# A fused FFT and two MLP layers: another order of all steps, and some tiles placed 8 bytes further on

## The chip, the cores and the metric

The program runs on one core of one Trainium2 chip. The metric is the device time of one execution in microseconds (us); lower is better. Engines are named as in the profile: PE is TensorE's matmul pipe and PEld its weight loads, DVE is VectorE, ACT is ScalarE, POOL is GpSimd, and SP is SyncE, which issues nearly all DMAs.

## The reference

```python
X = fft(fft(x, axis=1), axis=2); x = X.real          # x: (2, 3008, 256), then as 6016 tokens of 256
h = x @ w_in                                          # 256 -> 2048
x = (h * clip(h + 3, 0, 6) / 6) @ w_out               # 2048 -> 256
xn = x / sqrt(mean(x * x) + 1e-6) * rms_g
g = xn @ w_gate; v = xn @ w_val                       # 256 -> 1536 each
out = ((g * sigmoid(g)) * v) @ w_out2                 # 1536 -> 256
```

Weights arrive as 64-bit floats and are decoded on the chip.

## The kernel before

Every product is made of numbers split in two: a high part, rounded to the matmul's format (`F32R`), and a low part, the rest. Three matmuls (high by high, high by low, low by high) make one product. The low part is a subtraction, original minus high part, and it is the bulk of what GpSimd does.

**Stages.** (1) The inputs are folded by symmetry (`fold`), the Fourier matrices converted (`conv_mat`) and multiplied (`pmm`, `xmm`); the second batch does the same later (`late_fold`, `late_split`, `group`). The weights of the first layer are decoded meanwhile (`dec_win`, `wmm`, `dec_wout`). (2) The first layer runs as 96 items: six blocks of 1004 tokens (two halves of 502), 16 groups of hidden columns each. One item is 6 matmuls into the PSUM banks E and O, three DVE operations, two ACT ones (`L619`), two DVE ones (`L622`), one ACT cast of the high part (`L625`), two subtractions of 502 columns (one for each half, recorded at `L342`, the line of the helper `sub`) and 12 matmuls into four accumulators (`L640`). Two items are in flight on two pairs of E and O banks, so an item's first matmuls wait until the item two before it has passed `L622`. (3) The second layer runs as 72 chunks: six blocks of 12. A chunk is seven products of 3 matmuls (`prod`, steps a to g, `L796`), which share two banks; `hold` (`L803`, ACT) and `plus` (`L809`, DVE) read partial sums out of the banks, then come silu, products (`times`, `L817`), the cast (`high`, `L824`), the subtraction (`lows`) and two output groups of 6 matmuls (`outs`, steps v and w, `L839`). Before a block its rows are normalized (`rms`) and split (`split_j`); the second layer's weights are decoded during the last third of stage 2 (`dec_w2`) and combined and split (`sum_w2`, `split_w2`).

**Order.** Every function is a generator that yields between its operations, and the string `STEPS` names, one step at a time, which generator goes on. Within an engine instructions run in the order of this list. A bare number is a step of an item; `37g` is step g of chunk 37; other names stand in `TASKS`. A prime matters where the step holds a subtraction, sum or product that goes through `low[0]`: with the prime it runs on DVE, without it on POOL:

```python
low[0] = V if step != task else G
```

**Layout.** A tile's tag is its slot in SBUF. The subtraction's original lies in tiles R0 to R2 (`[P, 2 * BL]`, two halves of 502 floats, so the second half starts 2008 bytes in), its high part in HI or LO tiles of `[P, 2, PB]` (PB = 504, second half 2016 bytes in). Decoded second-layer weights are staged in slots B0 and YB0 as four rows of 512 floats (`st`).

Of the kernel before, what the change touches and what calls it, by code (L numbers as in the profile page):

```python
# [24 lines left out]
BL = 502  # L25
# [89 lines left out]
    pq00 PQ110 mat12 dwo0 PQ111 mat12 pq00' dwo0 PQ012 mat12 dwo0' ev01 PQ112 ev01 dwi1 lwo1 0 ev11 dwi1 ev11 dwi1 1 0
    sx1 dwi1 sx1 sx1 0 dwi1 X10 1 0 dwi1 1 X11 lwi2 0 1 X12 lwi3 lwo3 wt1 0 1 pq01 0 2 evx1 1 0 evx1 wt1 dwo1 2 1 2 0
    wt1 1 wt1 wt1 dwo1 2 evx1 pq01 dwi3 2 1 dwi3 2 wt1 wt1 2 lwo2 3 g wt1 wt1 2 3 4 dwi3 2 3 dwi3 3 4 3 4 5 3 dwo1 3 4 5
    4 3 5 6 4 dwo1 4 5 3 6 dwo1 5 4 6 7 5 dwo1 6 7 7 5 4 dwi2 6 5 dwi2 7 8 dwi2 6 5 7 6 dwi2 6 9 8 7 8 7 6 9 8 7 9 8 9 7
    8 9 dwi2 8 10 9 8 7 11 10 9 10 9 8 11 10 dwi2 11 10 11 9 dwo2 11 10 dwo2 10 wt2 11 dwo2 12 10 g wt2 12 11 12 10 wt2
# [5 lines left out]
    28 26 27 25 26 28 28 26 29 lf1 27 lf2 28 27 26 29 28 27 29 30 28 lf2 29 28 27 30 29 28 30 31 29 30 29 28 31 31 29 30
    31 29 30 31 30 lf2 32 30 31 33 32 32 31 30 33 32 31 33 32 33 31 32 33 32 lf2 34 33 32 31 35 ls00 33 34 33 32 35 lf2
    34 lm01 35 33 34 ls00 35 34 35 34 36 34 35 gr00 36 34 36 35 36 34 35 ls10 36 gr00 lm02 ls10' gr00 37 36 36 38 37 37
    36 35 38 37 38 37 38 36 37 38 37 39 38 37 40 39 38 39 37 38 40 39 40 39 40 38 39 40 39 41 40 39 42 41 40 41 39 40 42
    41 42 41 42 40 41 42 41 43 42 41 44 43 42 43 41 42 44 43 44 43 44 42 43 44 43 45 44 43 gr10 45 44 45 44 45 43 lm10
    gr10 45 ls01 gr10 lm11 46 pq10 45 pq10' 47 45 46 44 47 45 46 ls01 47 46 45 47 46 47 46 48 46 47 gr01 48 47 48 46 47  # L130
    48 46 lm12 gr01 48 ls11 gr01 49 48 48 47 49 49 48 ls11' 49 50 gr01 gr01 gr01 gr01 gr01 gr01 lm12 lm12 lm12 lm12 lm12
    lm12 ls11 ls11 ls11 ls11 ls11 ls11 pq10 pq10 pq10 pq10 pq10 pq10 46 46 46 46 46 46 46 46 46 46 46 46 47 47 47 47 47
    47 47 47 47 47 47 47 49 50 48 48 48 48 48 48 48 48 48 48 48 48 49 50 49 50 50 49 gr11 lo00 lo00 50 lo10 lo10 rms0 50
    rms0' 51 gr11 50 rms0 gr11 gr11 gr11 gr11 pq11 49 49 49 49 49 49 49 49 rms0' 51 do00 pq11 pq11 pq11 pq11 pq11 51 51
    rms0 51 50 50 50 50 50 rms0 do10 rms0 51 do00 rms0 51 52 rms0' 53 51 52 52 51 51 51 51 52 rms0 52 rms0 rms0 53 52 54
    53 52 53 54 52 52 52 52 52 53 rms0 53 54 rms0 53 55 54 55 rms0 54 53 53 53 53 53 55 54 55 rms0 54 55 56 54 56 55 54
    54 54 54 56 55 56 56 55 57 rms0 56 rms0 rms0 rms0 55 55 55 55 56 57 rms1 57 56 57 rms1' 58 57 rms1 rms1 58 56 56 56
    56 57 58 57 58 58 57 rms1 57 57 57 57 do00 rms1 do10 58 rms1 58 rms1 59 rms1' 58 59 60 59 58 58 58 58 59 rms1 59
    rms1 rms1 60 59 61 60 59 60 61 59 59 59 59 59 60 rms1 60 61 rms1 60 62 61 62 rms1 61 60 60 60 60 60 62 61 62 rms1 61
    62 63 61 63 62 61 61 61 61 63 pq12 62 63 rms1 62 63 64 pq12 pq12 pq12 pq12 pq12 64 63 62 62 62 62 64 64 rms1 rms1  # L140
    rms1 hj00 63 64 65 hj01 63 65 64 63 65 hj00 hj00 65 65 64 63 63 63 66 sj01' 64 66 67 65 66 hj01 hj01 66 64 64 64 64
    67 65 66 65 67 sj03 67 65 65 65 65 67 66 do00 do00 hj04 66 hw07 lg00 lg00 68 67 hj04' hj04 66 68 66 66 66 66 68 67
    68 do10 dg00 67 68 69 69 hw07 hw07 68 67 67 67 67 69 68 69 69 68 70 do10 do10 69 70 lg10 lg10 hw08 68 68 68 68 69 70
    70 69 70 hw08 hw08 71 70 71 dg10 69 69 69 69 70 71 71 70 71 72 dg00 71 72 71 70 70 70 70 72 72 71 72 73 dg00 72 dg10
    71 71 71 71 72 73 73 72 73 dg00 dg00 74 73 hw00 lv00 lv00 hw00 hw00 74 72 72 72 72 73 74 73 74 74 73 dv00 75 dg10 74
    75 73 73 73 73 74 75 75 74 75 76 dg10 dg10 75 76 lv10 lv10 74 74 74 74 hw01 75 76 76 75 76 hw01 hw01 77 76 77 75 75
    75 75 dv10 dv00 76 77 77 76 77 78 dv00 77 76 76 76 76 78 77 78 78 77 78 79 dv00 dv00 78 79 77 77 77 77 lo01 lo01
    hj03 78 79 79 78 79 80 hj03 hj03 79 80 sj02 78 78 78 78 80 79 80 80 79 81 80 sj04' 81 hj05 80 79 81 81 80 81 79 79
    79 hj05 hj05 82 dv10 82 83 81 dv10 82 81 80 80 80 80 82 83 81 82 81 81 81 81 83 82 83 dv10 dv10 82 83 lo11 lo11 hw05
    84 82 83 84 82 82 82 82 83 84 84 83 84 hw05 hw05 85 84 85 sw01 83 83 83 83 85 84 hw03 85 sw03' 84 85 hw04 86 86 sw02  # L150
    85 84 84 84 84 86 hw04 hw04 hw02 86 sw04' 85 86 hw06 87 85 87 86 85 85 85 85 87 hw06 hw06 87 87 86 88 hw02' hw02 87
    86 88 86 86 86 86 88 87 88 hw03' hw03 87 88 hj06 hj02 89 hj06 hj06 88 89 87 87 87 87 hj02' hj02 88 89 do01 89 88 89
    do11 90 do01 89 88 88 88 88 90 89 90 90 89 90 91 do01 90 do11 89 89 89 89 90 91 91 90 91 92 do01 do01 do11 hw17 lg01
    lg01 91 90 90 90 90 hw17 hw17 92 91 do11 do11 91 92 lg11 lg11 93 92 91 93 91 91 91 91 dg01 92 dg01 92 93 dg11 92 94
    93 93 92 92 92 92 92 dg01 93 94 93 94 95 94 93 94 93 93 93 93 dg01 dg01 94 95 lv01 lv01 hw10 94 95 95 0a 94 95 0b
    hw10 hw10 1a 0h 95 0i 0c dg11 0d 0j 95 0k 1b dv01 0e dg11 94 94 94 94 0l 95 0m 1h dg11 dg11 1i hw11 lv11 lv11 dv01
    1j 0f hw11' hw11 0g 0n 1c 0o 0r 1d dv01 1k 95 0p 0s 0q 95 95 95 dv01 dv01 1e 0v 0t 1l 0u 1m 1f 0w 1n hw18 lo02 lo02
    1r hw18' hw18 1g 1s dv11 2a 1o 2b dv11 1p 1v 2h 1q 2i 1t 2c dv11 2j 1u 2d 2k 3a dv11 dv11 1w lo12 lo12 3h hw15 hw15'
    hw15 2e sw11' 3c 2l sw13' hw13 3b sw12' hw14 2f 2m hw13 hw13 3k hw12 2n 2g sw14' 2r 3e hw12' hw12 hw16 4a 2s 2o 3l
# [822 lines left out]
```

## Time and profile before

| | before |
|---|---|
| median of 3 runs | 1064.54 us (1064.09 to 1066.43) |
| the profiled execution | 1065.55 us, its span 1063.8 us |
| mean granted clock of TensorE | 0.992 |
| PE busy | 1010.9 us (95%), 4356 matmuls |
| DVE, ACT, POOL busy | 829.7, 667.7, 510.0 us |
| DVE, ACT, POOL instructions | 1278, 1081, 424 |

The span runs from the program's first instruction to its last; about 1.8 us of the profiled execution lie around it. A matmul's end is modelled, so PE's idle time and the pace of its starts say more than its busy share. Idle time of the other engines costs nothing by itself.

### The profile page before, as it was taken

To read this page: it belongs to the slowest core of one execution; us is meant where nothing else is said; L and a number is where in the kernel's file an instruction comes from. 1 tells how busy PE (TensorE), PEld (TensorE's weight loads), DVE (VectorE), ACT (ScalarE), POOL (GpSimd) and SP (SyncE) were. 2 spreads that over 40 slices of the span, in tenths; PEclk is the share of its full clock that TensorE was granted. 3 is DMA by queue.
4 is the path that set the end of the run, shared out by engine and by line. 5 is a ranking of instruction groups with operands and counts; after the bars stand their busy time and mean duration, and the time that the engine had idled before them with its cause. 6 is when DMAs were issued, how large, how long until landed. Compare 5 with 4: busy or idle time off the path is not lost.

```text
span 1063.8 us, 12508 instructions
## 1 busy us (share of the span) xinstructions
PE 1010.9 (95%) x4356; PEld 817.9 (77%) x4356; DVE 829.7 (78%) x1278; ACT 667.7 (63%) x1081; POOL 510.0 (48%) x424
## 2 busy tenths in 40 slices
...
GB/s 284 162 180 1 83 5 113 1 87 10 172 27 1 51 49 40 59 40 82 57 98 1 78 1 1 42 36 1 1 78 1 1 59 20 1 1 39 1 1 39
DMA packets 22119, 53.28 MB, mean 50 GB/s; under 512 B 4326, under 2 KB 9958, under 8 KB 21678
## 3 DMA queue, kind: packets, MB, share of 16 engines
...
## 4 chain that ended last, share of the span: by engine, by line
PE 63%; DVE 23%; ACT 4%; issue 4%; DMA 2%; POOL 2%; SPq 0%; POOLq 0%; DVEq 0%; ACTq 0%
PE E L796 17%; PE acc L839 16%; PE O L796 12%; PE acc L640 11%; DVE R L622 5%; DVE T L611 3%; PE E L607 3%; DVE E L613 3%; PE O L607 2%; DVE O L614 2%; POOL LO L342 1%; DMA J<-in_x 1%; DVE B L342 1%; ACT R L619 1%; ACT HI L625 1%
## 5 line engine op out<-in xcount | busy, mean ns | idle before, releaser
L342 POOL TENSOR_TENSOR LO<-R,HI 128x502 fp32r<-128x502 f32 x192 | 240.8, 1277 | 125.3 <-ACT HI L625 125.3
L640 PE MATMUL acc<-HI,B 128*128 128x502 f32 x768 | 249.8, 390 | 1.3 <-POOL B L342 1.2
L640 PEld LDWEIGHTS acc<-HI,B 128*128 128x128 f32 x768 | 144.6, 188 | 32.1 <-POOL B L342 1.6
L342 POOL TENSOR_TENSOR HI<-R,HI 128x502 fp32r<-128x502 f32 x72 | 86.9, 1208 | 171.6 <-ACT HI L824 101.6
L640 PE MATMUL acc<-LO,B 128*128 128x502 f32 x384 | 151.0, 393 | 3.8 <-POOL LO L342 3.8
L342 POOL TENSOR_TENSOR LO<-R,LO 128x502 fp32r<-128x502 f32 x72 | 88.2, 1225 | 127.4 <-ACT LO L824 58.9
L625 ACT CAST HI<-R 128x1004 fp32r<-128x1004 f32 x96 | 99.5, 1038 | 71.6 <-DVE R L622 49.4
L809 DVE TENSOR_TENSOR R<-R,O 128x502 f32<-128x502 f32 x144 | 96.3, 674 | 31.1 <-PE O L796 25.8
L813 ACT ACTIVATE R<-R 128x502 f32<-128x502 f32 x144 | 88.6, 623 | 45.7 <-DVE R L809 44.0
L619 ACT ACTIVATE R<-E,c_three 128x502 f32<-128x502 f32 x96 | 65.2, 679 | 81.3 <-DVE E L613 67.4
L607 PE MATMUL E<-J,A 128*128 128x502 f32 x288 | 84.1, 401 | 10.8 <-DVE R L622 8.1
L803 ACT COPY R<-E 128x502 f32<-128x502 f32 x144 | 82.0, 573 | 16.1 <-PE E L796 11.6
L640 PEld LDWEIGHTS acc<-LO,B 128*128 128x128 f32 x384 | 72.3, 188 | 22.0 <-POOL LO L342 7.3
L607 PE MATMUL O<-J,A 128*128 128x502 f32 x288 | 82.8, 396 | 0.3 <-DVE A L390 0.3
L809 DVE TENSOR_TENSOR T<-T,O 128x502 f32<-128x502 f32 x48 | 32.3, 673 | 54.8 <-ACT T L803 53.1
L607 PEld LDWEIGHTS E<-J,A 128*128 128x128 f32 x288 | 54.9, 194 | 25.8 <-DVE R L622 12.0
L824 ACT CAST LO<-R 128x502 fp32r<-128x502 f32 x72 | 44.1, 612 | 46.5 <-DVE R L817 46.1
L622 DVE SCALAR_TENSOR_TENSOR R<-R,E 128x502 f32<-128x502 f32 x96 | 64.5, 672 | 8.9 <-ACT R L619 8.8
L613 DVE TENSOR_TENSOR E<-T,O 128x502 f32<-128x502 f32 x96 | 65.6, 683 | 7.3
L614 DVE TENSOR_TENSOR O<-T,O 128x502 f32<-128x502 f32 x96 | 65.1, 678 | 0.0
L607 PEld LDWEIGHTS O<-J,A 128*128 128x128 f32 x288 | 55.3, 192 | 12.3 <-DVE A L390 0.7
L619 ACT ACTIVATE R<-O,c_three 128x502 f32<-128x502 f32 x96 | 64.5, 672 | 0.0
...
## 6 DMA issues: line engine op xcount, KB each, us to landing
...
```

Of the source, the lines that this page charges most:

```text
L342: low[0].tensor_tensor(o, a, b, op=ALU.subtract)
L607: T.matmul(bk[:, :BL], a[:, lw, eo, fs], j[:, eo, lx], start=(n == 0), stop=(n == 2))
L613: V.tensor_tensor(E[:, :BL], t, O[:, :BL], op=ALU.add)
L614: V.tensor_tensor(O[:, :BL], t, O[:, :BL], op=ALU.subtract)
L619: S.activation(x, bk[:, :BL], AF.Relu, bias=c3)
L622: V.scalar_tensor_tensor(x, x, 6.0, bk[:, :BL], op0=ALU.min, op1=ALU.mult)
L625: S.copy(hi, r.rearrange("p (h n) -> p h n", h=2))
L640: T.matmul(acc[k][:, :BL], w[:, lw, f % 4, d * P:(d + 1) * P], (hi, lo)[lx][:, hf], start=(first and n == 0), stop=(last and n == 2))
L796: T.matmul(bk[:, :BL], w[:, lw, fs], j[:, lx], start=(n == 0 and m in (0, 1, 3)), stop=(n == 2), skip_group_check=True)
L809: V.tensor_tensor(c["t"][m], c["t"][m], c["b", 1][:, :BL], op=ALU.add)
L813: S.activation(t, t, AF.Silu)
L839: T.matmul(acc2[p, m][d][:, :BL], w[:, lw, cs], h[:, lx], start=(f == 0 and n == 0), stop=(f == NF2 - 1 and n == 2))
```

## The change

All 3678 steps are the same ones and stand in another order; the engine of some subtractions and products changes with the primes. The list itself is too long to print; these are its start, the stretch around the first late fold and its end, in both versions. Late folds are `lf`; `lf0` and the beginning of `lf1` stand some items earlier.

```diff
 STEPS = """
-    one dm x01 x01 raw00 xq x00 x00 lwi0 raw01 raw02 x02 x02 raw11 raw10 fold1 fold1 fold1 fold1 fold1 mat00 mat00 fx
-    fold1 mat00 sx0 fold0 fold1 fold0 sx0 fold1' sx0 fold0 X00 fold1 fold0 fold1 fold0 dwi0 fold1' fold0 dwi0 fold0
+    one dm x00 x00 raw01 x01 x01 raw00 raw11 xq fold0 x02 fold0 fold0 x02 fold0 fold0 mat01 lwi0 fold0 mat01 mat01 fold1
+    raw02 fold0 fold1 fold0' raw10 fold1 fold1 fold1 mat00 g mat00 fold1 PQ000 mat00 fold0 fold1 PQ100 fx fold0 sx0
...
-    16 17 15 16 17 16 dwo3 18 16 17 19 dwo3 18 18 17 16 19 17 18 19 dwo3 18 19 17 18 19 18 lf0 20 19 18 21 20 lf0 19 18
-    21 20 19 21 20 19 lf0 21 20 x11 lf0 22 20 lf0 20 21 22 20 23 21 22 21 20 pq02 23 21 23 22 pq02 23 22 21 23 22 22 lf1
+    17 16 17 16 14 17 18 14 14 18 17 lf0 17 x11 15 18 lf0 lf0 19 16 19 17 16' 16 16 19 17 18 18 17 17 lf1 18 19 lf1 18
+    19 20 20 18 19 21 20 19 20 18 21 19 20 21 22 21 lf1 20 19 22 x12 20 21 20' 22 23 21 23 22 21 20 22 pq02 21' pq02 23
...
-    70g 70n 69w 70o 70r 70p 70s 71c 70q 71b 71k 70v 70t 71i 70u 71j 71d 70w 71e 71l 71m 71f 71g 71n 71o 71r 71s 71p 71v
-    71q 71t ev5o0 71u ev5o0 ev5o0 71w ev5o1 ev5o0 ev5o0 ev5o1 ev5o1 ev5o1 ev5o1
+    69g 71h 70g 69o 71c 70o 69p 71b 69q 70p 67v 71k 71i 70q 71j 71d 69r 71e 69s' 68v 71l 71m 71f 70r 69v 71n 70s 70v 71r
+    71s 71g 71v 71o 71p 67w ev5o0 71q ev5o0 ev5o0 68w 69t 69u' 69w 70t 70u' ev5o0 ev5o0 70w 71t 71u' 71w ev5o1 ev5o1
+    ev5o1 ev5o1 ev5o1
 """
...
-    xqt = sl("c_xq", [TC, NCH, 4, 4])
+    xqt = sl("c_p9", [TC, NCH, 4, 4])
...
-        r = sl(rr("R", 2), [P, 2 * BL])
-        rh = (r[:, :BL], r[:, BL:])
+        r = sl(rr("R", 2), [P, 2, PB])[:, :, 2:]
+        rh = (r[:, 0], r[:, 1])
...
-        S.copy(hi, r.rearrange("p (h n) -> p h n", h=2))
+        S.copy(hi, r)
...
-            stage[tag, c] = sl(tag, [P, 4, 512])
+            stage[tag, c] = sl(tag, [P, 4, 516])[:, :, 2:514]
...
-        sq = sl("H1" if p else "HI2", [P, 2, BL])
-        for k in range(2):
-            S.activation(sq[:, k], y[k], AF.Square)
-        yield
-        v, r = sq[:, 0], sq[:, 1]
+        sq = sl("H1" if p else "HI2", [P, 2 * BL + 2])
+        v, r = sq[:, 2:PB], sq[:, PB:]
+        for k, t in enumerate((v, r)):
+            S.activation(t, y[k], AF.Square)
+        yield
...
-            c["r"] = sl(RT[k % 3], [P, 2, BL])
+            c["r"] = sl(RT[k % 3], [P, 2, PB])[:, :, 2:]
```

Read off the two lists, operations that go through `low[0]`, old and new:

| kind | on DVE | on POOL |
|---|---|---|
| an item's two subtractions | 0 to 29 | 192 to 163 |
| a chunk's two subtractions (`lows`) | 0 to 68 | 144 to 76 |
| of `rms` | 49 to 23 | 11 to 37 |
| `split_j` and `split_w2` | 44 to 28 | 25 to 41 |
| first folds | 6 to 2 | 0 to 4 |
| the others | 29 to 29 | 29 to 29 |
| all | 128 to 179 | 401 to 350 |

DVE instructions that stand ahead of the first matmul of an item: of item 5 113 and now 111, of item 20 212 and now 222, of item 30 280 and now 287. Ahead of item 20 stood 1 instruction of a late fold and now 12. The matmuls ahead of items 20 and 30 are the same in number, 492 and 660. The DVE instructions from item 50 to item 95 are 289 and now 298, from chunk 18 to chunk 66 352 and now 375.

With the layout, both halves of R lie 8 bytes past a multiple of 16, counted from the slot's start (before: the first at 0, the second at 2008, which is 8 past one). The HI and LO tiles stay at 0 and 2016, both multiples of 16. The staged weights move from 0 to 8 past such a multiple, and so does v, the first operand of `rms`'s products.

## Rows read from the trace of the kernel before

**Rows 1.** Busy time of each engine by stretch; (x) instructions; PEclk granted clock.
```profile
core 0: us, PE busy (x) PEld busy (x) DVE busy (x) ACT busy (x) POOL busy (x), PEclk, DMA share, GB/s
95.00:225.00 130.00, 124.12 (x543) 101.04 (x542) 124.25 (x192) 77.81 (x109) 87.36 (x69) 1.00 0.20 50
300.00:480.00 180.00, 176.09 (x762) 142.46 (x762) 168.78 (x269) 118.99 (x171) 130.84 (x107) 1.00 0.11 36
480.00:625.00 145.00, 137.76 (x575) 107.05 (x574) 121.71 (x188) 100.39 (x176) 55.56 (x44) 0.99 0.18 58
625.00:1040.00 415.00, 414.99 (x1807) 337.56 (x1806) 264.97 (x390) 259.05 (x467) 155.39 (x132) 1.00 0.05 18
1040.00:1064.00 24.00, 17.10 (x70) 12.31 (x68) 10.38 (x14) 9.59 (x17) 7.03 (x6) 0.94 0.11 44
```

**Rows 2.** Waits of PE in 95:225, 300:480, 480:625, 1040:1064; total us, times, longest.
```profile
...
PE E L607 <- DVE R L622: 5.6, 5, 1.9
...
PE acc L640 <- POOL LO L342: 3.8, 7, 0.8
...
PE E L796 <- ACT R L803: 2.5, 3, 1.1
...
PE acc L839 <- POOL LO L342: 1.5, 2, 0.8
PE acc L839 <- ACT LO L824: 0.8, 1, 0.8
PE E L796 <- ACT c_p L803: 0.7, 1, 0.7
```

**Rows 3.** GpSimd by line and shape; busy us, mean ns, then idle before.
```profile
...
L342 POOL TENSOR_TENSOR W<-W 128x502 f32<-128x502 f32 x8 | 8.6, 1075 | 4.6 <-DVE W L342 4.6
...
L342 POOL TENSOR_TENSOR YB<-B,YB 128x512 fp32r<-128x512 f32 x4 | 5.2, 1294 | 0.0
```

**Rows 4.** Timeline of GpSimd in 312:318 and 655:668; start us, us.
```profile
...
312.14 1.27 POOL L342 TENSOR_TENSOR LO<-R,HI 128x502 fp32r<-128x502 f32 x1 [1.55 <-ACT HI L625]
313.38 1.27 POOL L762 TENSOR_TENSOR R<-R,HI 128x502 f32<-128x502 f32 x1
314.60 1.07 POOL L342 TENSOR_TENSOR LO<-R,HI 128x502 fp32r<-128x502 f32 x1
...
662.25 1.08 POOL L342 TENSOR_TENSOR LO<-R,LO 128x502 fp32r<-128x502 f32 x1
663.28 1.08 POOL L342 TENSOR_TENSOR W<-W 128x502 f32<-128x502 f32 x1
```

**Rows 5.** VectorE by line and shape, and its subtractions of L342 (min/median/max ns).
```profile
...
L817 DVE TENSOR_TENSOR R<-R,E 128x502 f32<-128x502 f32 x72 | 48.6, 675 | 17.6 <-PE E L796 17.5
L817 DVE TENSOR_TENSOR R<-R,c_p 128x502 f32<-128x502 f32 x24 | 24.4, 1015 | 11.0 <-ACT R L813 11.0
...
L342 DVE TENSOR_TENSOR J<-W,J x9: 668/682/683, 578.5 to 936.2; 128x502 fp32r<-128x502 f32 x9
```

**Rows 6.** ScalarE's cast of an item, and one that reads two runs (timeline).
```profile
...
L625 ACT CAST HI<-R 128x1004 fp32r<-128x1004 f32 x96 | 99.5, 1038 | 71.6 <-DVE R L622 49.4 <-PE acc L640 20.3 <-PE O L607 0.8
...
39.77 1.03 ACT L586 CAST J<-PQX 128x1004 fp32r<-128x1004 f32 x1 [1.07 <-DVE PQX L532]
```

**Rows 7.** Late folds on VectorE in 150:200, by line and shape.
```profile
...
L408 DVE TENSOR_TENSOR PQ<-PQ 126x1024 f32<-126x1024 f32 x3 | 4.4, 1453 | 0.0
L406 DVE TENSOR_TENSOR W<-PQ 126x1024 f32<-126x1024 f32 x3 | 3.9, 1316 | 0.0
...
L417 DVE TENSOR_TENSOR B<-W 126x256 f32<-126x256 f32 x8 | 3.0, 418 | 0.0
```

**Rows 8.** Two more stretches, columns as in the first group.
```profile
...
0.00:15.00 15.00, 0.73 (x2) 0.51 (x3) 7.78 (x21) 5.53 (x7) 0.94 (x5) 1.00 0.85 251
...
550.00:575.00 25.00, 23.53 (x93) 17.90 (x92) 22.81 (x36) 17.61 (x32) 8.23 (x7) 0.93 0.07 22
```

**Rows 9.** Timeline of TensorE at 560.
```profile
...
560.90 1.46 PE L796 MATMUL O<-B,B 128*128 128x502 f32 x3
```

More of the change, by code (lines that the diff above doesn't have):

```diff
@@ L115 @@
[L115 to L119, printed above, removed]
@@ L125 @@
[L125 to L129, printed above, removed]
@@ L130 @@
[L130 to L159, printed above, removed]
@@ L165 @@
-    dv12 dv12 6u hw25 rms2 ly1 ly1 7e rms2 hw25' hw25 6w 7l rms2 sw21' rms2 7f sw23' hw23 8a sw22' hw24 8b hw23' hw23
-    hw22 sw24' 8h hw22' hw22 hw26 8c hw24' hw24 8k hw26' hw26 8e rms2' 7m 8l rms2 7g 7n rms2 8f 7o 7r rms2 9a 8i 7p 9b
-    9h 7q 8d 8j 7s 9i 7t 9c 8m 9j 7v 7u 8n 9k 8r rms2 7w 8s rms2 rms2' 8g rms2 9d 8o 9e rms2 8p 8v rms2 rms2 rms2 9l
-    hj10 8q 9f rms3 9m hj10 hj10 10a 9n 8t 9g rms3' 9r 8u 10b 10h 9o rms3 10c 10i 9s 9p 8w 10j rms3' 10k 9q rms3 hj11
-    10d rms3 hj11' hj11 10e 9t rms3 9v 10l 9u rms3 10m 10f rms3' 9w rms3 10n rms3 10g 10r rms3' 11a 10s 10o 11b 10p rms3
@@ new lines @@
+    58 59 rms1 58 58 58 58 60 59 do10 do10 rms1 59 60 lg10 lg10 60 rms1 61 60 59 59 59 59 59 61 60 dg00 dg10 60 61 61 60
+    rms1 61 60 60 60 60 rms1 hw08 rms1 61 hw08' hw08 rms1 dg00 62 61 62 rms1 63 62 61 62 61 61 61 61 63 rms1 pq12 63
+    rms1 63 rms1 62 rms1 62 64 63 rms1 62 64 63 65 rms1 65 64 62 62 62 62 62 rms1 64 63 65 63 63 64 65 rms1 rms1 rms1
+    rms1 64 66 pq12' pq12 pq12 pq12 pq12 63 63 63 64 65 64 66 67 hj00 67 hj01 hj00 hj00 64 64 64 64 65 66 hj01 hj01 66
+    67 65 66 65 65 65 65 65 66 sj01' dg10 67 sj03 67 68 66 hj04 68 67 69 dg00 dg00 66 68 hw00 lv00 lv00 66 66 66 66 67
@@ new lines @@
+    68 69 68 67 69 hj04 hj04 67 67 67 67 68 hw00' hw00 dv00 68 69 69 68 70 70 69 68 68 68 68 dv00 69 70 70 69 70 71 dv00
+    70 72 71 70 71 69 69 69 69 71 70' 71 72 70 70 70 70 71 dg10 72 71 72 72 71 73 dg10 dg10 72 73 71 71 71 71 lv10 lv10
+    hw01 72 73 73 72 73 hw01 hw01 74 73 74 72 72 72 72 dv00 dv00 dv10 73 74 lo01 lo01 74 73' 74 75 75 74 73 73 73 73
+    dv10 74 75 75 74 75 76 76 75 74 74 74 74 dv10 75 76 76 75' 76 77 77 76 75 75 75 75 dv10 dv10 76 77 hw05 lo11 lo11 77
+    76 77 78 hw05 hw05 77 78 79 sw01' 77 78 hw03 76 76 76 76 78 77 79 78 hj03 hw03 hw03 79 hj03 hj03 77 77 77 77 78
@@ new lines @@
+    sw03' 79 sj02 79 hw04 78 80 79 sj04' 78 80 hj05 81 80 hj05 hj05 80 78 78 78 78 81 79 80 79 81 sw02 79 80 hw04' hw04
+    81 80 81 79 79 79 sw04 83 83 82 81 80' 83 hw02 81 80 80 80 80 83 82 81 83 hw06 hw02 hw02 82 81 81 81 81 83 hw06 hw06
+    82 83 82 hj06 84 hj02 hj06 hj06 82 84 85 83' 82 84 84 82' 82 82 82 82 85 84 85 83 83 83 83 85 hj02' hj02 85 do01
+    do11 86 do01 84 86 85 87 84 86 84 84 84 84 84 87 85 86 87 85 86 85 85 85 85 87 do01 87 86 do01 do01 88 86 87 lg01
+    lg01 88 86 86 86 86 86 88 87 88 88 87 dg01 89 do11 88 89 90 dg01 88 89 87 87 87 87 89 88 90 89 90 88 88 88 88 89
@@ new lines @@
+    dg01 90 89 90 hw17 89 91 90 91 hw17 hw17 92 91 90 91 89 89 89 89 92 90 91 92 92 90 90 90 90 do11 dg01 dg01 91 92
+    hw10 91 93 92 91' hw10 hw10 93 91 91 91 91 93 93 92' 92 93 94 do11 do11 93 94 lg11 lg11 92 92 92 92 lv01 lv01 93 94
+    94 93 94 95 94 95 93 93 93 93 dg11 94' 94 95 dv01 95 dg11 94 94 94 94 95 dg11 95 dv01 95' 0a 95' 0b 0h dg11 dg11 95
+    0i hw11 lv11 lv11 dv01 0j hw11' hw11 95 95 95 dv01 dv01 0c 0d 0k 1a 1b 1h 0e 1i 1c 0l lo02 lo02 1j 1d 0m 1k 0f hw18
+    1e 0n hw18 hw18 0g 1l 0r 2a 1m dv11 1f 0s' 2h dv11 1g 0v 1n dv11 1r 0o 3a dv11 dv11 0p 2b 1s' hw15 lo12 lo12 2c 0q
@@ new lines @@
+    1v hw15 hw15 2i 2k 0t 1o 2j 0u' 2d 1p sw11' 0w 3h 1q hw13 sw13' 1t 3b hw13' hw13 hw14 2e 1u' 3c hw14 hw14 3i 2l 1w
+    2m 3j 3k sw12' 2f sw14' hw12 2g hw12' hw12 hw16 2n 3e hw16 hw16 2o 2r 3d 3l 2s 4a 2p 3m 3f do02 2q 4b do12 do02 4h
+    3g 3n 2t 4c 3o 3r 2u 2v 4i 4k 3p 3s' 4j do02 4e do12 2w 4l do02 do02 do12 4d hw27 lg02 lg02 3q 4f hw27 hw27 4m 3t 3v
+    4n do12 do12 4r 5a 3u' hw28 lg12 lg12 4s 5b 5h dg02 4g 5i 4v dg02 5j 4o 5d dg02 4p 5c hw28' hw28 dg12 dg02 dg02 3w
+    5k dg12 hw20 lv02 lv02 hw20' hw20 5e dg12 6a 5l 4q 6b 6h dg12 dg12 4t 5f 6i lv12 lv12 hw21 4u 6c 5m 6j 6d 5n dv02
@@ new lines @@
+    hw21 hw21 5g 6k 5r dv02 6e 5s 4w 5o 6l 5p 6m dv12 6f dv02 dv12 7a 6g dv02 dv02 7h 5q 7b ly1 6o 5t 5v 6n 6p 5u 7i 6r
+    7c dv12 7j 7d 6s' 7k 5w rms2 6q dv12 dv12 6t rms2' 7e ly1 ly1 hw25 6u' 6v rms2 hw25' hw25 7l rms2' 6w sw21' sw23'
+    hw23 rms2 sw22' hw24 8a 7m rms2 hw24 hw24 7f hw22 8h rms2 7g 8b sw24' rms2 hw22' hw22 hw26 8c rms2 7n 8k 7o 9a 7r
+    hw26' hw26 8e 7p 7s 8i 9h 9b 8l rms2 9c 8j 7q 8f rms2 hw23' hw23 9k 7v 9i rms2 7t 8n 9j 8d 7u' 8r 7w rms2 8s 8m rms2
+    8g rms2' 9e rms2 8v 8o 9l rms2 8p rms2 rms2 rms2 9d hj10 8q rms3 9f hj10' hj10 10a 8t 9m rms3 10b 10h 9n 9g 8u' rms3
@@ new lines @@
+    14h 13q 12p ev0o1 14c 12q 13t ev0o1 ev0o1 14b 14k 13u 13f 12t 14i 14e 12u' 14j 14d 13n 14l 12w 13r ev0o1 ev0o1 14m
+    13s 14f 13v 14n 14r 14g rms4 14s 13w 14o rms4' 14p 14v rms4 14q rms4 14t 15a 14u' 16a 15h 14w 16h 15c 16c 15k rms4
+    16k 15e rms4 16b 15l rms4 15b 16i rms4 15f 15i 16j rms4 16e 15j 15d 16l rms4 16d 15n rms4 16f 15m 15r rms4 16m 17a
+    15s' 15g 17h rms4 15v 15o rms4 16n 15p 17c rms4' 16r 16g 15q 17k 16s 17b 15t 16o 17e rms4 16p 18a 17i 17l 16q 18b
+    17j 15u' 16t 17d rms4 18h 17f 17m 16u hj20 16v 18i hj20 hj20 17n 18j 18d 17r rms4 rms4 rms4 17g 17s rms5 15w 17o 17p
@@ new lines @@
+    31n 29w rms7 31o 31r rms7 31p 32c 31s' 32b rms7 32k 31v 30u' rms7 31q 30w sj31 32i 31t 32j 32e 31u' hj33 33a rms7
+    rms7 rms7 32l 31w hj33 hj33 33h sj33' 32f sj32 33b 32n 33c hj32 sj34 33i 32r 34a 33j hj32 hj32 33d 34h 32d 33k 32s'
+    34c 32m 32v 34k 34e 32g 34l 33e 32o 34f 33l 32p 34b 33m 33f 32q 34i 33g 32t 33n 34j 34d 32u 33o 33r 35a 34n 33p 35b
+    34m 33s hj34 32w 34r 33q 35h hj34 hj34 33t 35i 34g hj35 33u 33v 35j 34o 34s 34p 33w 34q hj35 hj35 34t 34v 34u' ly4
+    34w 35d 35c 36a 35k hj36 36b 36h hj36 hj36 35e 36i 36c 35l ly4 ly4 36j 36d 35m 36k 35f 35g 35n 36e 35o 35r 37a 36l
@@ new lines @@
+    35s 35p 37b 36m 37h 35v 35q 37i 35t ev2o0 37d 35u' 37j ev2o0 ev2o0 37c 35w 37k 37e 36f ev2o0 ev2o0 37l 36g 37m 37f
+    36n 36o 37g 36r 37n 36p 38a 37o ev2o1 38b 37r 36s' ev2o1 39a 37p 36q 38h 36v 37s ev2o1 36t 38i 37q 37v 38j 36u'
+    ev2o1 ev2o1 37t 39h 37u 38c 36w 38k 37w rms8 rms8 38e 38d 38l rms8 39b 38m rms8 38f 39i 38g 38n 39j 39d 38o 38r 40a
+    38p 38s 39c 40h 38q 38v 39k 38t 38u 39e 40b 39l 38w 39m 40i 39f 40j 39g 39n 40d 39o 39r 40c 39p 39s 41a 40k 39q 39v
+    41h 39t 39u 41c 40e 41k 39w 40l 40m 41b 40g 41i 40f 40o 41j 41d 40n 40p rms8 40q 40r 42a rms8 40s' 41e 40t rms8 40v
```

150 lines of the change are left out of this document (75 added, 75 removed).

## The prediction, made before the changed kernel ran

> **What bounds the kernel now.** I read the stretches first [rows 1]: PE's idle time in each is its length less PE busy. From 625 to 1040 us it is 415.00 − 414.99 = 0.01 us: the second layer is paced by PE alone, one matmul each 415 / 1807 = 0.230 us, and nothing in the change removes a matmul. So a gain has to come from the other stretches. Their idle time: 95 to 225 us 5.9, 300 to 480 us 3.9, 480 to 625 us 7.2, 1040 us to the end 6.9 us, 23.9 in all. Before 95 us more is lost, in the loads and folds.
>
> Then the waits, to see who ends these [rows 2]. In 95:225 it is DVE: 5.6 us in five waits for `L622`, the last reader of the banks E and O, and DVE is busy 124.25 of 130 us [rows 1]. So DVE paces this stretch; PE only shows it. In 300:480 it is POOL: 3.8 us in seven waits of `L640` for the low part. In 480:625 many small waits of the first chunks, ACT's bank reads the largest (2.5 us). At the end 1.5 + 0.8 + 0.7 = 3.0 us in the last chunk's chain; the rest of the 6.9 is the last output.
>
> **The 8 bytes.** Does a place matter to POOL? The trace has pure cases. W<-W subtracts halves 2008 bytes apart, so one operand is 8 past a multiple of 16 where the other is on it: 1075 ns. YB<-B,YB has both on multiples of 16: 1294 ns for 512 columns [rows 3]. In an item the first half has both on multiples (1.27 us), the second has R 8 off (1.07) [rows 4]. So an operand pair 8 apart costs 0.20 us less, and after the change both halves are such pairs. DVE's subtraction does not care: J<-W,J contains both kinds and lies between 668 and 683 ns [rows 5].
>
> Under "GPSIMD Engine Reference", Performance versus the Vector engine, the Trainium skill gives one price for a two-input operation, about 2.6 cycles an element at 1.2 GHz, whatever the place: 502 × 2.6 / 1.2 = an estimate of 1.09 us. The trace agrees for the pairs 8 apart and contradicts it for the others; by the page alone the layout would save nothing.
>
> What the 0.20 us is worth: in stage 2 the low part ends the 3.8 us of waits [rows 2], seven of them, 0.54 us each. The first half's 0.20 us comes off each; where a subtraction now goes to DVE (28 of them before the chunks) the pair runs side by side and 1.07 − 0.68 = 0.4 us more goes. I take −2 of the 3.8 us; bounds 0 (DVE becomes late in its place, below) and −3.8. The cost of the new layout: ACT's cast now reads two runs of 502; L586 does that at 1.03 us against 1.038 of L625 [rows 6], nothing. The slots B0 and YB0 grow by 64 bytes, paid with the slot of `xqt`, which moves into c_p9. The next to write there is the last converted matrix piece, and it waits only for the three small DVE operations of `fx`, in both lists long before; if that cover were gone, one DVE step, about 1 us.
>
> **The order, DVE's stretch.** Ahead of item 20 eleven more late-fold instructions stand: two of 1.45, one of 1.32, four of 0.42 us [rows 7], and two combining steps and two memsets, an estimate of 2 us together: 7.9 us. Four subtractions of items add 4 × 0.68 = 2.7; four first folds (0.68 each) and one subtraction of a `dec_wout` (twice as wide, some 1.2) leave: −3.9. Sum +6.7 us of DVE for the same 492 matmuls. What waits behind it is each item's `L611`, `L613` and `L622`, and the matmuls two items on. DVE has 5.75 us idle in 95:225. If all of it could be filled, +1 us; if none, +6.7. I take +3.5. POOL's queue gets the folds instead, at a time when it is idle (0.94 of the first 15 us busy [rows 8]).
>
> **The start.** Loads stand in another order on SP's queue: x00 first, raw00 behind x01. Ahead of raw00's end lie 1008 + 558 + 1008 + 558 KB and the 512 KB of `dm`, 3.6 MB; the first 15 us move 251 GB/s × 15 us = 3.8 MB [rows 8]. So the first folds start as before and the first product is later, but DVE has the same work ahead of item 5 (113 and 111 instructions) and is what item 5 waits for. I take 0; bounds ±4, about half of the 7.2 us that DVE is idle in these 15 us.
>
> **The hand-over, 480 to 625 us.** 7.2 us of idle, and slow matmuls: in 550:575 the granted clock falls to 0.93 [rows 8]; after the waits three matmuls take 1.46 us there [rows 9] instead of 0.7, which is 1.2 in place of 2.4 GHz, and 0.07 of 25 us is 1.8 us. Together 9.0. For the first 18 chunks I added up, for every two matmul groups that share a bank, the ACT or DVE work which the list puts between them, and took off the matmul time between. Example: the old list has `8c`, `hw24'`, `hw24`, `8k`, `hw26'`, `hw26`, `8e`: no matmul between c and e, though k must read the bank in between; the new one puts `9a`, a product, there. The shortage falls from 36 to 18 us. If the idle time falls as the shortage, half of 9.0 goes: −4.5. Bounds −8 and +3 (DVE carries 17 subtractions of these chunks now).
>
> **The end.** The new list holds back 67w, 68w, 69w and 70w until the last products are out: 24 × 0.23 = 5.5 us of matmuls beside 71's chain o, p, q, t, u, five operations no dearer than the 1.0 us of `L817` [rows 5]. Of the 3.0 us of waits 2.5 go; bounds 0 and −3.
>
> **The saturated part.** DVE gets 23 more instructions between chunks 18 and 66 and is idle 150 of 415 us there; PE's own work covers them. But bank reuse has less room, one product instead of two between steps g and the next but one b. +1 us for that; bounds 0 and +5.
>
> **Sum.** −2 + 3.5 + 0 − 4.5 − 2.5 + 1 = −4.5 us. Against the profiled execution's own 1065.55 us that is 1061.05 us; the median of the runs lies 1.0 us under it, so 1064.54 − 4.5 = **1060.0 us**. About 0.2%, 2.1 us, can be told from no change.
>
> **Rivals.**
>
> *DVE's price is covered, 1055 us, chance 0.18.* The folds fill DVE's idle 5.75 us (+1 in place of +3.5), and the hand-over falls by 7. Speaks for it: faster POOL subtractions hold DVE up less. Against: DVE was 96% busy in 95:225.
>
> *DVE becomes the bound, 1071 us, chance 0.19.* Place: items 10 to 95. The late folds cost the full 6.7 us, and from 300 to 480, where DVE is busy 168.8 of 180 us, nine more instructions of 0.7 us between items 50 and 95 bring another +3 beyond what POOL's waits give back; only the end gains: 6.7 + 3 − 2.5 = +7. It decides once DVE's idle time in 300:480 falls under some 5 us. Speaks for it: an operation of DVE with two SBUF inputs runs into POOL's: `L817` takes 675 ns with one input in PSUM and 1015 with both in SBUF [rows 5], and all 51 added operations are of that kind. Under "Advanced Engine Details and Errata", VectorE Performance Modes, the Trainium skill says that the second SBUF port of VectorE is shared with GpSimd and the two block each other; the 1015 ns agree.
>
> *Nothing to measure, 1064 us, chance 0.13.* DVE's +6.7 and the gains cancel.
>
> *The layout does nothing, 1063 us, chance 0.04.* If the 0.20 us were a matter of how POOL's spans are recorded, POOL's waits would stay and −2 would go. Against: starts follow at the same difference. 313.38 − 312.14 = 1.24 us after an operation of the slow kind, 663.28 − 662.25 = 1.03 after one of the fast kind [rows 4]. Under "Perfetto Trace Analysis", GPSIMD Engine Instruction, the Trainium skill calls GpSimd's spans unreliable and wants start-to-start spacing; the spacing says the same here.
>
> **Numbers.** The forecast, 1060.0 with its own range 1054 to 1064, has 0.46. Faster by over 0.2%: 0.40 of it and the first rival, 0.58. Within: 0.05 of it, 0.13 and 0.03, 0.21. Slower: 0.21. The range of 8 in 10 reaches into the first two rivals: 1051 to 1070.
>
> **What would show it.** POOL's LO<-R,HI at about 1.07 us wherever no DVE operation is in its way. The number of PE waits for POOL in 300:480 down from seven. DVE busy over 125 of 130 us in 95:225, and item 30's first matmul some 3 us later. PE idle in 480:625 about 4 us; PE's waits in the last 20 us under 1. The prediction is wrong if item 30 comes much earlier or over 7 us later, or if the second layer, now without a wait, gets some.

## The result, and the profile after

The changed kernel takes 1046.34 us (median of 4 runs, 1046.17 to 1048.50); the kernel before, run beside it, 1065.49 us (4 runs, 1064.09 to 1066.46). The ratio is 0.9826, 95% interval 0.9807 to 0.9845: about 19 us faster. The forecast was 1060.0 with a range of 1051 to 1070, so the sign was right, and the gain was four times the forecast and outside the range. The profiled execution took 1046.17 us, its span 1044.4 us, the mean granted clock 0.992 as before, so the clock does not explain the gain. Single stretches differ: the granted clock is 0.94 after and 1.00 before in 130:160, 1.00 after and 0.93 before in 550:575.

A line of the page after (busy us, share of the span, instructions):

```profile
...
PE 1002.1 (96%) x4356; PEld 820.1 (79%) x4356; DVE 837.5 (80%) x1329; ACT 667.6 (64%) x1081; POOL 424.0 (41%) x373
```

PE has the same 4356 matmuls. GpSimd lost 86 us of work and DVE gained only 7.8 us, though it has 51 more instructions. Next the stretches after, columns as in [rows 1]:

```profile
95.00:225.00 130.00, 124.78 (x538) 101.76 (x537) 123.33 (x200) 79.15 (x111) 67.25 (x60) 0.99 0.16 42
300.00:480.00 180.00, 178.36 (x775) 144.97 (x775) 173.27 (x282) 121.54 (x176) 117.86 (x104) 1.00 0.10 33
480.00:625.00 145.00, 143.38 (x622) 115.91 (x621) 122.94 (x206) 108.06 (x192) 45.26 (x39) 1.00 0.18 59
625.00:1020.00 395.00, 394.80 (x1727) 323.41 (x1726) 261.77 (x392) 250.53 (x450) 127.42 (x109) 1.00 0.06 19
```

From 480 to 625 us PE is idle 1.6 us instead of 7.2, and it issues 622 matmuls in place of 575: 47 more, at 0.23 us each 10.8 us of progress in that stretch alone. DVE is busier in 300:480 (173.27 against 168.78) and PE is nevertheless idle only 1.6 us there, before 3.9.

The waits of PE after, in 95:225, 300:480, 480:625 and 625:1020 (total us, times, longest); from 1020 us to the end the view lists none:

```profile
PE E L608 <- DVE R L623: 4.0, 3, 1.7
PE acc L641 <- DVE LO L343: 1.3, 1, 1.3
...
PE E L608 <- DVE R L623: 1.1, 2, 0.8
...
PE E L797 <- ACT R L804: 0.6, 1, 0.6
PE O L797 <- DVE c_p L810: 0.4, 1, 0.4
PE E L797 <- DVE B L343: 0.4, 1, 0.4
...
PE acc L840 <- POOL LO L343: 0.2, 1, 0.2
```

Beside [rows 2] (line numbers are one higher): the seven waits for POOL in 300:480 are gone, those of the hand-over shrank to 0.4 to 0.6 us each, and the 3.0 us at the end are gone.

**Where the time came from.** Waits alone do not add up to 19 us, so I kept a ledger: the start of the first matmul of a step, less the matmul time that the list puts ahead of it (0.2285 us for each matmul of 502 columns, 0.232 for 512, 0.173 for 378, the pace of undisturbed starts). What this difference grows by from one step to the next is what PE lost between them, at whatever cause, stretches at half clock included. The last column is the span less 985.5 us, the sum of all matmuls.

```
us lost by PE   to item 20   20-40   40 to 0a   0a to 18a   18a to 71g   71g to end    all
before              44.0       3.7       6.1        14.0         3.4          7.1      78.3
after               48.2      -0.3       3.0         3.3         0.6          4.1      58.9
difference          +4.2      -4.0      -3.1       -10.7        -2.8         -3.0     -19.4
```

Step 0a is the first product of the second layer, 18a that of chunk 18, 71g the last product; 0a to 18a is the hand-over. More than half of the gain lies there.

**What GpSimd's operations did.** By line and shape, and one tile's subtractions (min/median/max ns), after:

```profile
L343 POOL TENSOR_TENSOR LO<-R,HI 128x502 fp32r<-128x502 f32 x163 | 185.0, 1154 | 169.3 <-ACT HI L626 162.0 <-issue 4.3 <-DVE R L623 2.9
...
L343 POOL TENSOR_TENSOR LO<-R,HI x163: 1064/1076/2086, 61.9 to 482.1; 128x502 fp32r<-128x502 f32 x163
```

The median is now 1076 ns for both halves, as W<-W had it in [rows 3]. The trace of layout_only (one of the experiments below: the old list on the new layout) has the case that tells what matters, the place of one operand or that of the two together. Its sums of staged weights (`sum_w2`, 512 columns wide) have both operands 8 bytes past a multiple of 16:

```profile
L711 POOL TENSOR_TENSOR B<-B 128x512 f32<-128x512 f32 x2 | 2.6, 1294 | 0.1
```

Before, with both on a multiple, the same two took 1300 ns. So it is the distance between the two operands that counts, not the place of one.

**What DVE's operations did.** The products `times` after, to be read beside [rows 5]:

```profile
L818 DVE TENSOR_TENSOR R<-R,E 128x502 f32<-128x502 f32 x72 | 48.4, 673 | 17.5 <-PE E L797 17.3
...
L818 DVE TENSOR_TENSOR R<-R,c_p 128x502 f32<-128x502 f32 x24 | 18.1, 754 | 5.3 <-ACT R L814 5.2
```

With one operand in PSUM nothing changed (675, now 673 ns); with both in SBUF the mean fell from 1015 to 754 ns at the same size. The reason is in the timeline of before, of GpSimd and then of DVE around 620 us (start us, us):

```profile
619.36 1.28 POOL L342 TENSOR_TENSOR HI<-R,HI 128x502 fp32r<-128x502 f32 x1 [6.21 <-ACT HI L824]
...
619.94 1.24 DVE L817 TENSOR_TENSOR R<-R,c_p 128x502 f32<-128x502 f32 x1 [0.69 <-ACT R L813]
621.18 0.42 DVE L755 TENSOR_SCALAR H<-H 128x502 int32<-128x502 int32 x1
```

GpSimd ends at 620.64, DVE at 621.18, 0.54 us later. There are 72 products of this kind in before, these 24 and 48 of `R<-R,T`, and they divide cleanly: 36 met no GpSimd operation and took 666 to 683 ns; 2 saw one begin after them, 674 ns; 34 began while one ran, took 1264 ns in the mean, and each ended 0.54 us (536 to 544 ns) after it. So such a DVE operation waits until GpSimd is through. After, 17 of 72 began so and their mean is 976. What follows the wait goes with the width: five DVE operations of 1024 columns in before end 1.08 to 1.09 us after GpSimd's. I call this excess DVE's wait for GpSimd and added it up for all of DVE's operations that end like this: 42.5 us in before, of which 6.0 between item 40 and 0a and 9.8 in the hand-over; 24.4, 6.0 and 1.7 us after. Such sums hang by about 1 us on which operations are counted. Under "SBUF — State Buffer", Terms, the Trainium skill says that VectorE and GpSimd take a pair of ports in turn, one of them for a full instruction while the other is blocked altogether; the trace agrees for a VectorE operation that comes second, and adds the 0.54 us. It agrees the other way round too: after, 47 of the items' and chunks' subtractions on GpSimd began while a DVE operation with two SBUF inputs ran, and took 1514 ns in the median; the 140 with no such operation in their way took 1076. So a subtraction moved to DVE can still hold up the ones left on GpSimd.

### The profile page after: what moved, and what is told of

The parts are those of the page before. It is cut to its first block, busy times and chain, and to the rows that moved or that the text cites. A ratio compares the mean times of both kernels' runs of the same rounds, so it can differ in the third digit from the quotient of the medians.

```text
span 1044.4 us, 12417 instructions
## 1 busy us (share of the span) xinstructions
PE 1002.1 (96%) x4356; PEld 820.1 (79%) x4356; DVE 837.5 (80%) x1329; ACT 667.6 (64%) x1081; POOL 424.0 (41%) x373
## 4 chain that ended last, share of the span: by engine, by line
PE 74%; DVE 18%; ACT 3%; issue 2%; DMA 2%; POOL 1%; SPq 0%; DVEq 0%; ACTq 0%
PE acc L840 18%; PE E L797 18%; PE acc L641 15%; PE O L797 13%; PE E L608 4%; DVE R L623 3%; PE O L608 3%; DVE T L612 2%; DVE E L614 2%; DVE O L615 2%; DMA J<-in_x 1%; POOL LO L343 1%; DVE W L338 1%; DVE LO L343 1%; ACT R L620 1%
## 5 line engine op out<-in xcount | busy, mean ns | idle before, releaser
L343 POOL TENSOR_TENSOR LO<-R,HI 128x502 fp32r<-128x502 f32 x163 | 185.0, 1154 | 169.3 <-ACT HI L626 162.0
L343 POOL TENSOR_TENSOR HI<-R,HI 128x502 fp32r<-128x502 f32 x39 | 46.4, 1189 | 106.0 <-ACT HI L825 92.5
L343 POOL TENSOR_TENSOR LO<-R,LO 128x502 fp32r<-128x502 f32 x37 | 42.8, 1158 | 103.8 <-ACT LO L825 94.6
L623 DVE SCALAR_TENSOR_TENSOR R<-R,O 128x502 f32<-128x502 f32 x96 | 64.2, 669 | 0.0
L818 DVE TENSOR_TENSOR R<-R,E 128x502 f32<-128x502 f32 x72 | 48.4, 673 | 17.5 <-PE E L797 17.3
```

What stands on the lines that cost most here:

```text
L343: low[0].tensor_tensor(o, a, b, op=ALU.subtract)
L623: V.scalar_tensor_tensor(x, x, 6.0, bk[:, :BL], op0=ALU.min, op1=ALU.mult)
```

## The experiments

Twelve kernels, in four groups, each group beside its own runs of before. Differences between kernels of two groups are taken from the ratios; the ledger is of each one's profiled execution.

```
                  median us (range)             ratio to before [95%]
order_only        1059.35 (1057.51-1061.97)     0.9941 [0.9921, 0.9961]
layout_only       1061.06 (1060.99-1061.57)     0.9956 [0.9937, 0.9974]
old_engines       1061.49 (1060.47-1067.74)     0.9959 [0.9939, 0.9979]
new_engines       1083.87 (1082.79-1084.36)     1.0164 [1.0142, 1.0187]
new_then_old      1057.90 (1056.70-1059.05)     0.9916 [0.9894, 0.9939]
old_then_new      1052.99 (1050.88-1056.07)     0.9874 [0.9847, 0.9901]
both_slow         1063.25 (1061.63-1064.97)     0.9967 [0.9955, 0.9979]
old_tail          1051.77 (1049.69-1052.84)     0.9858 [0.9837, 0.9879]
old_spread        1061.67 (1060.64-1062.32)     0.9957 [0.9940, 0.9974]
items_only        1053.19 (1052.56-1054.99)     0.9878 [0.9863, 0.9893]
chunk_dve         1054.28 (1051.54-1056.06)     0.9883 [0.9867, 0.9900]
no_lows           1064.79 (1060.78-1066.47)     0.9960 [0.9941, 0.9979]

us lost by PE   to item 20   20-40   40 to 0a   0a to 18a   18a to 71g   71g to end    all
order_only          48.2      -0.1       8.7         5.7         4.0          4.1      70.6
layout_only         44.6       3.4       5.1        11.8         1.8          6.9      73.7
old_engines         47.8      -0.3       8.1         6.9         6.3          5.3      74.1
new_engines         46.2       8.8      10.0        18.6         6.4          6.5      96.5
new_then_old        47.0      -0.3       3.1        13.0         1.2          7.0      71.0
old_then_new        44.2       3.5       6.9         4.0         0.7          4.2      63.5
both_slow           52.8       1.2      10.6         5.0         4.0          4.1      77.7
old_tail            48.0      -0.3       3.1         3.2         2.8          7.0      63.7
old_spread          43.9       3.6       5.1        12.0         1.7          6.9      73.3
items_only          48.1      -0.2       3.7         5.6         3.9          4.2      65.3
chunk_dve           49.2      -0.3       3.0         5.1         5.9          4.2      67.2
no_lows             47.0       4.3       6.2         9.9         2.8          8.1      78.3
```

**order_only and layout_only: the two parts of the change by themselves.** order_only is before with the new list, primes included; layout_only is the changed kernel with the old list.

> The new list of steps on the old layout (both halves of R, the staged weights and rms's v where they were). Theory 'places': the order brings nearly all of the 19 us, since the 10.8 us between chunk 0 and chunk 18 went with waits for bank reads by ACT and DVE, which no POOL duration touches; 1047 to 1051 us. Theory 'layout': the low parts' 0.20 us carry the gain, also because VectorE runs less into GpSimd; then this is 1056 to 1064 us.

> The old list of steps on the new layout. Theory 'places': only the waits of PE for POOL go (3.8 us in 300:480, 1.5 at the end), and VectorE's two-input operations wait a little less; 1059 to 1063 us. Theory 'layout': 1048 to 1056 us.

The new list alone is worth 0.59%, 6.3 us, the layout alone 0.44%, 4.7 us; together they are worth 1.74%, 18.5 us. order_only fell into the range of theory 'layout', layout_only into that of 'places', so neither theory holds for both. 7.5 us belong to neither part alone (each ratio is known to some 2 us). The ledger puts most of these into the items: from item 40 to 0a the new list alone loses 2.6 us more than before, the layout alone 1.0 less, both together 3.1 less. The waits of PE in 300:485, first of order_only, then of layout_only:

```profile
PE acc L641 <- POOL LO L343: 3.2, 6, 0.8
...
```

```profile
PE acc L640 <- POOL LO L342: 2.2, 5, 0.7
...
```

Neither removes PE's waits for the low part; both together do. DVE's waits for GpSimd from item 40 to 0a are 6.0 us before, 9.1 with the list alone, 4.8 with the layout alone, 6.0 with both.

**old_engines and new_engines: who does the subtractions.** old_engines has the new order and layout, with each operation on its old engine; new_engines the old order, the new layout and the new choice. The edits only move primes, step by step, from one list to the other.

> The new order and layout, but each operation that goes through low[0] on the engine that it had in the old list (128 on VectorE, 401 on GpSimd). Theory 'places': the order of the steps alone does it, 1046 to 1050 us. Theory 'engines': the 97 low parts of items and chunks that now run on VectorE shorten the chains for which the new order leaves room, and without them the new order stalls: 1054 us or more.

> The old order on the new layout, with the engines of the new list (179 on VectorE, 350 on GpSimd). Theory 'engines': faster than the layout alone by several us, 1050 to 1056. Theory 'places': VectorE, 96% busy from 95 to 225 us and 94% from 300 to 480, gets subtractions at places where it has no room, so no faster than the layout alone and rather slower, 1060 to 1068 us.

Old engines cost 14 us of the 19: on the new layout the new order without its engines (0.9959) is worth no more than the old one (0.9956). New engines in the old order cost 17.5 us over before, more than either theory expected. So the move to DVE is no gain in itself, and neither is the order: the two fit each other. In the old order the new engines raise the hand-over to 18.6 us. PE's largest wait in new_engines in 480:640:

```profile
PE E L797 <- ACT R L804: 3.9, 6, 1.1
...
```

In the hand-over old_engines loses 6.9 us where the changed kernel loses 3.3; DVE's waits for GpSimd there are 8.6 against 1.7 us.

**new_then_old and old_then_new: which half of the order.** The first takes the new list up to 0a and the remaining steps in the old order with their old engines, the second the reverse. Both have the new layout.

> The new layout; the new list up to the first product of chunk 0, and from there the remaining steps in the old order with the old list's primes. If the gain of the hand-over (10.8 us between chunk 0 and chunk 18) lies in how the chunks' own steps stand, it is gone: PE's lag at chunk 0 as with the new list (51 us), rising by 11 to 14 us to chunk 18, and the whole 1059 to 1063 us. If it lies in what had been done ahead of chunk 0, the lag rises by 3 to 6 us only and the whole is 1048 to 1054 us.

> The new layout; the old list up to the first product of chunk 0, and from there the remaining steps in the new order with the new list's primes. If the chunks' own steps make the hand-over's gain: lag 53 us at chunk 0, some 57 at chunk 18, the whole 1048 to 1051 us. If the preparation ahead of chunk 0 makes it: 1056 us or more.

The hand-over follows the chunks' own steps (their order and engines together), not what the items leave behind: 13.0 with the old ones after new items, 4.0 with the new ones after old items. The times miss the ranges that went with this by 1 to 2 us, new_then_old from below (1057.9 us), old_then_new from above (1053.0).

**both_slow: the layout undone the other way.** The changed kernel with both halves of R on multiples of 16, as HI and LO are:

```diff
-        r = sl(rr("R", 2), [P, 2, PB])[:, :, 2:]
+        r = sl(rr("R", 2), [P, 2, PB])[:, :, :BL]
-            c["r"] = sl(RT[k % 3], [P, 2, PB])[:, :, 2:]
+            c["r"] = sl(RT[k % 3], [P, 2, PB])[:, :, :BL]
```

> The changed kernel with only R's two halves put back on multiples of 16 (0 and 2016 bytes), so that now both of an item's and a chunk's low parts have their operands alike: all at 1.27 us, the second half too. Theory 'layout is what the new order is fitted to': worse than the new order on the old layout (1059 us), where half were fast: 1062 to 1075 us. Theory 'the 0.20 us are hidden by now': 1047 to 1052 us.

```profile
L343 POOL TENSOR_TENSOR LO<-R,HI x163: 1244/1275/2285, 63.9 to 496.0; 128x502 fp32r<-128x502 f32 x163
```

The median goes from 1076 to 1275 ns for both halves, and 15 of the 19 us are gone. Whether the clock has a part in the 4.6 us that it loses more ahead of item 20 is not shown: 0.89 was granted in 130:160, 0.94 in the changed kernel, but old_tail, with 1.00 there, loses as much by item 20 as the changed kernel (48.0 and 48.2). From item 40 to 0a, at full clock, it loses 10.6 us against 3.0.

**old_tail: the last six chunks in the old order.** The new list up to 66a, then the old order and engines.

> The changed kernel up to the first product of chunk 66, and from there the remaining steps in the old order with the old primes. The held-back output groups 67w to 70w then stand where they did. Expected: the waits of PE near the end come back and the whole is 2 to 4 us over the changed kernel, 1048.5 to 1050.5 us. Rival: the tail's gain came from the faster low parts, and this is within 1 us of the changed kernel.

The waits of PE from 980 us to the end:

```profile
PE acc L840 <- POOL LO L343: 1.3, 2, 0.7
PE acc L840 <- ACT LO L825: 0.8, 1, 0.8
PE E L797 <- ACT c_p L804: 0.7, 1, 0.7
PE acc L840 <- POOL HI L343: 0.7, 1, 0.7
```

The old last chain is back; it costs 3.4 us by the ratios and 4.8 in the ledger, 2.9 of them behind 71g. layout_only, new_then_old and old_spread, which end as it does, lose 6.9 to 7.0 us there; the kernels that end in the new order with the new engines 4.1 to 4.2, with either layout.

**old_spread: one gap closed.** layout_only with some 30 steps around chunk 8 rearranged (the list is cut here), so that products stand in the gaps that the prediction named:

```diff
-    sw21' rms2 7f sw23' hw23 8a sw22' hw24 8b hw23' hw23 hw22 sw24' 8h hw22' hw22 hw26 8c hw24' hw24 8k hw26' hw26 8e
+    sw21' rms2 7f sw23' hw23 8a 7m sw22' hw24 7g 8b 8h hw23' hw23 hw22 sw24' hw22' hw22 7n 8c 8k hw26 hw24' hw24 9a 7o
```

> The old list on the new layout, with one stretch of 40 steps around chunk 8 put as the new list has it: 7m and 7g go ahead of 8b, 8h and 8k follow 8b and 8c at once, and 9a stands between 8c and 8e. In the run of the old list on the new layout these places cost PE 1.0, 0.9 and 0.4 us. Theory 'places': this one exchange takes PE's lag at chunk 12 down by about 2 us, and all of it arrives at the end: 1058.5 to 1059.5 us against 1061.1. Rival: VectorE, 98% busy from 525 to 550 us, is late for something else instead, and the lag at chunk 18 is the same: 1060.5 to 1062 us.

No gain: 12.0 us in the hand-over against 11.8. The 1.0, 1.2 and 0.5 us that layout_only loses behind 8b, 8c and 8e became 0.4 behind 8a and 0.8 each behind 8c, 8e and 8d. A gap closed in one place moved the loss to the next.

**items_only: the layout in the items alone.** order_only with only the items' R moved.

> The new list on the old layout, but with the items' R tile in its new place (the chunks' R, the staged weights and rms as before). The order alone loses 6 us more than the changed kernel from item 50 to chunk 0, in waits for POOL's low parts. If these are the first halves at 1.27 us, the lag at chunk 0 falls from 56.8 us to 51 or 52, and the whole is 1051 to 1054 us. If the staged weights' splits or rms on POOL hold the items up, it stays above 1056 us.

From item 40 to 0a it loses 3.7 us where order_only loses 8.7. In the items, the 0.2 us off the first half is what the new order lacked.

**chunk_dve: more of the same.** The changed kernel with all 144 low parts of the chunks on DVE.

> The changed kernel with all 144 low parts of the chunks on VectorE (68 there so far). VectorE gets 76 x 0.7 = 53 us more, 47 of it between chunk 18 and the end, where it is idle a third of the time. Theory 'PE covers it': 1045 to 1048 us, with fewer collisions with GpSimd. Theory 'places': the list's order leaves room for a low part on VectorE only where it has put one, and the bank reads that queue behind the others come late: 1050 to 1060 us, the loss spread over all chunks.

DVE's waits for GpSimd fall further, from 24.4 to 19.6 us, and the time rises by some 6 us: 1.8 more in the hand-over, 5.3 more behind it. DVE now has 76 subtractions of 0.7 us more in a list that was made without them.

**no_lows: GpSimd's part in the hand-over by itself.** Before, without the subtractions of chunks 0 to 17:

```diff
 def lows(k, m):
+    if k < 18:
+        return
 ...
-    T.matmul(acc2[p, m][d][:, :BL], w[:, lw, cs], h[:, lx], ...)
+    T.matmul(acc2[p, m][d][:, :BL], w[:, lw, cs], h[:, lx if k >= 18 else 0], ...)
```

> The kernel before, old order and old layout, but the 36 subtractions of chunks 0 to 17 are left out; the matmuls that would read the low part read the high part again, so PE has the same matmuls (the output lacks those low parts). In the hand-over 18 of DVE's operations with two SBUF inputs started in the trace of before while GpSimd ran, mostly one of these subtractions, and ended 0.54 us after it: 9.8 us of DVE waiting between the first products of chunk 0 and of chunk 18, where PE lost 14.0 us. Theory, the hand-over is lost largely to DVE's waits for GpSimd: they fall under 4 us, the loss falls from 14.0 to about 7, and the time is some 7 us under before (about 1059). Rival, the step order alone makes it (two products that share a bank with too little between them): the waits go from DVE and the loss stays at 11.5 or more, the time within 3 us of before.

It fell between the two. DVE's waits for GpSimd in the hand-over went from 9.8 to 2.2 us, PE's loss from 14.0 to 9.9, and the time by 0.40%, 4.3 us. (Its profiled execution had lost 3.6 us more by item 40, with a granted clock of 0.89 in 130:160, ahead of anything that the edit touches, and its end was 1.0 us longer; so its span shows no gain.) PE's two largest waits in 480:625 stand nearly as they were (2.5 and 2.2 us before):

```profile
PE E L796 <- ACT R L803: 2.6, 3, 1.1
PE O L796 <- DVE c_p L809: 1.7, 1, 1.7
```

So some 4 us of the old hand-over go with these subtractions, and not all 4 are DVE's waits. A wait of 0.7 us of PE itself for one of the low parts went too. And about 1 us is a stretch at half clock: in 550:575 the granted clock is 0.93 before and 1.00 in no_lows, and between 8a and 9a PE loses 3.8 us before, 2.7 in no_lows and 2.8 in layout_only, which has 1.00 there as well. By subtraction some 2 us remain for DVE's waits, an estimate. The other 10 stay without the subtractions; with the layout new in both, the new order and engines take 11.8 to 3.3.

## Why the prediction was wrong

The signs of most terms were right and the sum was a quarter of what came. Term by term, measured with the ledger. A measured number is what the stretch gained, from whatever cause:

```
term                          forecast   measured
8 bytes (items 40 to 0a)         -2        -3.1
DVE's stretch (to item 40)       +3.5      +0.2
the start                         0     in the line above
the hand-over                    -4.5     -10.7
the saturated part               +1        -2.8
the end                          -2.5      -3.0
sum                              -4.5     -19.4
```

**The step that failed first: "If the idle time falls as the shortage, half of 9.0 goes".** Both the 9.0 and the half were too small. The 9.0 came from PE's idle time and the slow clock; the ledger says 14.0. A matmul's span is 0.39 us in the mean where its pace is 0.2285, so the matmul ahead of a wait hides some 0.16 us of it. And the shortage does not scale the loss. Halved by the prediction's count, which no run measures, it left 3.3 of 14.0. The new list alone took 8.3; the layout, to which I gave nothing here, took another 2.4 (5.7 to 3.3; in the old order 14.0 to 11.8). About 1 us of each difference to the 14.0 is the stretch at half clock. On the new layout the new order with the old engines goes from 11.8 to 6.9, and only the new engines bring it to 3.3. The mechanism that the prediction named, too little between two groups that share a bank, is seen in PE's waits for ACT's bank reads, 2.5 us before and 0.6 after, but no run isolates it: old_spread closed one such gap, and the loss moved to the next. no_lows shows that a second stood beside it: DVE's waits for GpSimd, some 2 us, up to 4 with all that went with those subtractions.

**DVE's stretch.** The 6.7 us were priced with durations of before, and those contained waits for GpSimd: the 30 late-fold instructions took 20.9 us before and 16.9 after. Ahead of item 20 the forecast nearly holds: DVE had 148.2 us of work before and now 152.9 (the prediction makes it 155), and PE lost 4.2 us more by then. I forgot that work done earlier is not there later: ahead of item 40 it is 237.8 and 239.5 us, and PE is nearly level by item 30, 48.1 us of loss against 47.4. The start, forecast at 0, cost 2.1 us at item 5 and nothing at item 8. Two marks that the prediction set were therefore missed: item 30's first matmul came 0.7 us later and not 3, and DVE is busy 123.33 of 130 us in 95:225, not over 125.

**The 8 bytes.** The mechanism and its size per operation were right (both_slow takes it back, and the rival that the layout does nothing has fallen). Its worth was not: −2 was read off the waits of the old order, where the layout alone gives 1.0 us from item 40 to 0a, 4.7 in all. In the new order it gives 12 us (0.9941 to 0.9826), 5 of them in the items from 40 to 0a (8.7 to 3.7 in items_only). I added the parts as if they were independent; 7.5 us lay in that they were not.

**The saturated part.** The 0.01 us of idle time hid 3.4 us of small losses between 18a and 71g; over half of it went with the layout (1.8 in layout_only, 4.0 in order_only), but with the old engines in the new order it is 6.3 on the same layout. The cost that I expected of the tighter bank reuse is not seen: 0.6 us in all.

**The end.** Right in place and cause, and near in size; old_tail shows it.

**The rivals.** *DVE's price is covered* (1055) was nearest and still 9 us short; both its statements came true, the second by more than it said. *DVE becomes the bound* has fallen: DVE is idle 6.7 us in 300:480, and PE does not wait for it more than 1.1 us there. *Nothing to measure* has fallen as well. *DVE becomes the bound* may fit new_engines, though: the same engine choice in the old order is 1084 us.

What stays open: why the two parts fit each other so closely in the items is shown as far as PE's waits for the low part (3.2 us, 2.2 us, none) and DVE's for GpSimd (9.1, 4.8, 6.0) go; how much of the 7.5 us is the one and how much the other I did not separate. DVE's waits there are about the same before and after, so they alone do not explain it.
